# Even-odd token order, DMA transposes of keys and queries, and half of the normalising on ScalarE

## The chip, the core and the metric

The kernel runs on one core of one Trainium2 chip. The core has a matrix engine (TensorE, PE in the profile, its weight loads PEld), a vector engine (VectorE, DVE), a scalar engine (ScalarE, ACT), GpSimd (POOL) and SyncE (SP), which here only issues transfers. Sixteen DMA engines move the data. SP and ACT issue transfers on hardware queues, POOL on a software queue. Each engine works through its instructions in order and waits at an instruction until what it needs is there.

The metric is the device time of one execution in microseconds, median of several runs. Before the change it is 180.32 us (three runs, 180.05 to 180.48).

## The reference

Two stages follow one another. The first is attention over 4 batches of 8 heads, 768 tokens and 64 values a head. A token sees the 128 tokens that end with itself, and the first four tokens of the sequence (the sinks). The second is a gated block over the attention's output, 512 wide:

```python
keep = is_sink | in_window
scores = np.where(keep, scale * q @ k.T, -1e9)
a = softmax(scores);  x = a @ v                  # [B, S, 512] over the heads

h = gelu(x @ w_in);  u, v = halves of h          # 2 x 512
v_n = (v - mean(v)) / sqrt(var(v) + 1e-6) * g_ln
v_s = einsum('ts,bsd->btd', w_sg, v_n) + b_sg[None, :, None]
out = x + (u * v_s) @ w_out
```

The matrix `w_sg` (768 x 768) mixes tokens, so it and `b_sg` follow the order in which the kernel keeps the tokens.

## The kernel before

Two heads form a pair, and there are 16 pairs, four for each batch. Step n of the main loop (L571) scores pair n, while it also finishes pair n-1 and prepares pairs n+1 and n+2. All engines' orders are written out by hand: what the code issues first, an engine does first. There is no planner with costs; the only freedom is a list of fillers (below).

**Loads.** `load_qk` (L75) has SP load keys and queries of a pair, two transfers of 384 KB, in pieces of 1536 bytes (six consecutive tokens to a partition). There are two buffers of each. `load_v` (L85) has POOL load the values, 128 tokens to a tile, in pieces of 256 bytes, cast to bf16 on the way, into one of four buffers. `load_first` (L91) loads the first pair in halves on SP and ACT. `load_weights` (L159) is called at the start of each step: w_in in steps 0 to 3, w_sg in step 4, b_sg, g_ln and w_out in step 5, all on POOL's queue.

**Preparing a pair.** `repack` (L187) has POOL cast k and q to bf16 (`k_bf`, `q_bf`), two steps ahead. `keys` (L208) and `queries` (L216) turn them: six transposes of 128x128 on PE into PSUM (`cps`, L197), then one ACT copy into `kT` or `qT` (L204), which also puts the tokens back into order, since six consecutive tokens had lain in one partition. POOL then copies the sinks' keys from `kT` into `sk` (L214). In step n, `keys(n+1)` stands after the first scores, and `queries(n+1)` beside it up to step 3 and after the second scores from step 4 on. `prepare_first` (L221) does the same for pair 0 in halves.

**Attention.** `score` (L249) does a third of the scores of a pair on PE and their exp on ACT (L264); `keep_band` (L266) multiplies with a mask on DVE; `sinks` (L273) does the scores against the sinks. The score tiles have two PSUM buffers in all. `values` (L288) multiplies with v one token tile at a time; three tiles share one PSUM buffer `av`, of which there is one, and DVE normalises them together, a reciprocal (L315) and a multiply of 557 ns (L316) into `x`. The values of pair n-1 are done in step n.

**Turning x.** For pairs 4 to 6, 8 to 10 and 12 to 14 (`by_dma`, L280) SP issues a DMA transpose of x into `xT` (L321). The others are turned on PE and copied by DVE (`columns`, L283).

**The gated block.** After step 4, 8 and 12, `hidden` (L422) does the first matrix product of the batch that is finished (`hidden_v`, `hidden_u`), with gelu on ACT, and with half of the values of pair n in between. In the step after it, the second scores and `values` of the other half follow. It also fills the list `fillers`: after step 4 six `spatial_weights` (L177; PE turns w_sg by 128x128 blocks, DVE copies into `wsgT`), and for each batch eight `spatial` (L377; six matmuls `vs`, then on DVE `gv`, which needs g_ln and b_sg, and `gT`) and six `project` (L391; `o_ps`, then a DVE add or ACT copy and a store on SP). `spread` takes fillers off the list one or two at a time between the parts of steps 5 to 8 and so on. PSUM has two buffers for `vs`, `o_ps` and the hidden layers together.

After step 15 come the last values, the last hidden layer and the last batch's spatial and output products. A guard at the end checks the reciprocals' range and jumps to a slower, stable path (`stable_path`) if one is out of range; it is not run here.

Of the kernel before, what the change touches and what calls it, by code (L numbers as in the profile page):

```python
# [17 lines left out]
def kernel(  # L18
# [27 lines left out]
    assert 0 < n_sink <= 32  # L46
# [17 lines left out]
    NV = 4  # L64
    v_bufs = [consts.tile([128, 2, NT, 65], BF16, name=f"v_sb{i}") for i in range(NV)]
    kT_bufs = [consts.tile([128, S], BF16, name=f"kT{i}") for i in range(NB)]
    sk_bufs = [consts.tile([128, 128], BF16, name=f"sk{i}") for i in range(NB)]
    exs_bufs = [consts.tile([128, NS], BF16, name=f"exs{i}") for i in range(NB)]
# [6 lines left out]
    def load_qk(n):  # L75
        b, hp = divmod(n, HP)
        pair = []
        for src, name in ((k, "k_sb"), (q, "q_sb")):
            dst = loads.tile([128, 2, NT, 64], F32, name=name)
            nc.sync.dma_start(out=dst, in_=src[b, 2 * hp:2 * hp + 2].rearrange(  # L80
                "h (p t) d -> p h t d", t=NT))
            pair.append(dst)
        qk[n] = pair

    def load_v(n):  # L85
        b, hp = divmod(n, HP)
        nc.gpsimd.dma_start(  # L87
            out=v_bufs[n % NV][:, :, :, 0:64],
            in_=v[b, 2 * hp:2 * hp + 2].rearrange("h (t p) d -> p h t d", p=128))

    def load_first():  # L91
        pair = [loads.tile([128, 2, NT, 64], F32, name=name) for name in ("k_sb", "q_sb")]
        for a in range(2):
            for src, dst, queue in ((k, pair[0], nc.sync), (q, pair[1], nc.scalar)):
                queue.dma_start(
                    out=dst[:, :, HT * a:HT * (a + 1), :],
                    in_=src[0, 0:2, NH * a:NH * (a + 1)].rearrange(
                        "h (p t) d -> p h t d", t=HT))
# [10 lines left out]
    def band(dst):  # L109
        nc.gpsimd.memset(dst, 1.0)  # L110
        nc.gpsimd.affine_select(
            out=dst[:, 0:128], in_=dst[:, 0:128], compare_op=ALU.is_ge, fill=0.0,
            base=0, pattern=[[1, 128]], channel_multiplier=-1)
        nc.gpsimd.affine_select(
            out=dst[:, 128:256], in_=dst[:, 128:256], compare_op=ALU.is_ge, fill=0.0,
            base=-1, pattern=[[-1, 128]], channel_multiplier=1)
# [7 lines left out]
    for i in range(NB):  # L124
        nc.vector.memset(sk_bufs[i], 0.0)

    def copy_masks():
        nc.vector.tensor_copy(mask0, mask)
        for hl in range(2):
            nc.vector.memset(mask0[0:n_sink, 2 * hl, :], 1.0)  # L130
# [22 lines left out]
    g_sb = consts.tile([128, KU], F32, name="g_sb")  # L153
    b_bc = consts.tile([128, S], F32, name="b_bc")
    wsg_sb = consts.tile([128, NT, S], BF16, name="wsg_sb")
    w_out_sb = consts.tile([128, KU, DM], BF16, name="w_out_sb")
    wsgT = consts.tile([128, NT, S], BF16, name="wsgT")

    def load_weights(n):  # L159
# [6 lines left out]
        elif n == 4:  # L166
            for c in (slice(0, HT), slice(HT, NT)):
                nc.gpsimd.dma_start(
                    out=wsg_sb[:, c, :],
# [508 lines left out]
```

## Time and profile before

| | us |
|---|---|
| median of three runs | 180.32 |
| the profiled execution | 180.66 |
| its span in the profile | 178.8 |
| PE busy | 156.6 |
| DVE busy | 146.0 |
| ACT busy | 119.4 |
| POOL busy | 57.5 |

All times below are microseconds from the start of the span. The stages are: the first pairs up to 33, the first hidden layer up to 45.5, steps 5 to 8 up to 75, the second hidden layer up to 87, steps 9 to 12 up to 113, the third hidden layer up to 125.5, steps 13 to 15 up to about 141, then the last values, hidden layer, spatial and output products.

A line of the timeline or of the chain begins with its start and its length. The chain of waits follows the work that ended last back to the start, at each step to what released it. In a line such as "x2" the instructions of a group are merged. "SPq" and "DMA_DIRECT2D" on POOL are the time in which the engine issues a transfer, not the time in which the data moves; "to landing" counts from the issue to the last byte.

### The profile page before, as it was taken

Reading aid. Unit: us, or ns where it says so; the run is one execution under the profiler, and the core shown is the slowest. Engines: PE = TensorE matmul, PEld = TensorE weight load, DVE = VectorE, ACT = ScalarE, POOL = GpSimd, SP = SyncE. Lnnn points to the kernel's source line nnn. Section 1 sums busy time; section 2 is a strip of 40 time slices with the busy share of each in tenths; the row PEclk is TensorE's granted clock in tenths of the full one; section 3 lists DMA queues with packets and bytes.
Section 4 is the critical chain, followed back from the end, with each engine's and each line's share of the span. In section 5 each row is a group of like instructions: output and inputs, shape, how many; then the busy total and the mean of one; then the engine's idle time right before and its main releaser. Section 6 shows DMA issues by size and latency. Waiting matters only on the chain.

```text
span 178.8 us, 3744 instructions
## 1 busy us (share of the span) xinstructions
PE 156.6 (88%) x1407; PEld 88.7 (50%) x1418; DVE 146.0 (82%) x359; ACT 119.4 (67%) x168; POOL 57.5 (32%) x98
## 2 busy tenths in 40 slices
PE   0769779799689999899899999899799999999970
PEld 0447556345556555445456545355465554555430
DVE  5665989599889999698999998699999948858950
ACT  2488999867938668666968668877986856640000
POOL 8459999950042060425006070550010000000000
PEclk9999999999999999999999999999999999999999
DMA  5999999999857739895285969986202241011072
GB/s 158 266 306 265 267 271 273 191 207 218 103 179 48 202 66 209 303 270 39 20 219 33 214 183 192 380 108 44 44 4 44 50 178 59 0 63 60 0 294 66
DMA packets 47974, 27.24 MB, mean 152 GB/s; under 512 B 33680, under 2 KB 44944, under 8 KB 47952
## 3 DMA queue, kind: packets, MB, share of 16 engines
q0 software_dynamic: 27904, 6.31, 37.5%
q1 hardware_dynamic: 19504, 20.26, 37.5%
q10 hardware_dynamic: 544, 0.39, 0.7%
q8 instruction: 12, 0.20, 0.5%
q14 instruction: 10, 0.08, 0.1%
HBM read 24.81 MB, written 6.29 MB: 174 GB/s over the span
## 4 chain that ended last, share of the span: by engine, by line
PE 75%; ACT 12%; issue 4%; DVE 4%; DMA 2%
PE vs L383 17%; PE hu L345 13%; PE o_ps L397 11%; PE hv L333 11%; ACT ex L264 7%; PE sc L260 7%; PE cps L197 5%; PE av L305 4%; ACT kT L204 3%; PE scs L275 2%; PE av L308 2%; DMA k_sb<-in_k_dram 2%; ACT qT L204 2%; PE av L311 1%; DVE ex L271 1%
## 5 line engine op out<-in xcount | busy, mean ns | idle before, releaser
L264 ACT ACTIVATE ex<-sc 128x1024 bf16<-128x1024 f32 (+1 forms) x48 | 45.6, 958 | 16.9 <-PE sc L260 16.7
L383 PE MATMUL vs<-wsgT,vn 128*128 128x384 bf16 x192 | 35.5, 327 | 0.5 <-DVE wsgT L182 0.4
L191 POOL CAST k_bf<-k_sb 128x768 bf16<-128x768 f32 x15 | 12.3, 823 | 42.7 <-DMA k_sb<-in_k_dram 31.8
L397 PE MATMUL o_ps<-w_out_sb,gT 128*128 128x512 bf16 (+1 forms) x93 | 23.8, 370 | 1.2 <-DVE o_sb L401 0.8
L271 DVE TENSOR_TENSOR ex<-ex,mask 128x1024 bf16<-128x1024 bf16 x32 | 23.0, 722 | 1.8 <-ACT ex L264 1.7
L333 PE MATMUL hv<-w_in_sb,xT 128*128 128x512 bf16 x92 | 22.2, 379 | 1.9 <-DVE xT L286 1.7
L383 PEld LDWEIGHTS <-vn 128*128 128x128 bf16 x192 | 17.9, 98 | 12.0 <-issue 1.2
L345 PE MATMUL hu<-xT,w_in_sb 128*128 128x384 bf16 x128 | 23.2, 325 | 0.1
L260 PE MATMUL sc<-qT,kT 64*128 64x256 bf16 x192 | 19.0, 280 | 2.2 <-DVE qT L240 1.3
L386 DVE SCALAR_TENSOR_TENSOR gv<-vs,g_sb,b_bc 128x384 bf16<-128x384 f32 x32 | 19.5, 611 | 1.7 <-PE vs L383 1.7
L348 ACT ACTIVATE uT<-hu 128x384 bf16<-128x384 f32 x32 | 15.7, 490 | 6.5 <-PE hu L345 6.3
L337 DVE BATCH_NORM_STATS2 st<-v_all 128x6 f32<-128x512 f32 x24 | 16.3, 677 | 4.6 <-ACT v_all L335 4.5
L335 ACT ACTIVATE v_all<-hv 128x512 f32<-128x512 f32 x24 | 14.3, 597 | 7.2 <-PE hv L333 6.9
L316 DVE TENSOR_TENSOR x<-av,inverses 128x384 bf16<-128x384 f32 x32 | 17.8, 557 | 1.1
L305 PE MATMUL av<-v_sb,ex 128*128 128x65 bf16 x192 | 18.2, 198 | 0.2 <-DVE x L316 0.2
L305 PEld LDWEIGHTS <-ex 128*128 128x128 bf16 x192 | 14.5, 100 | 7.2 <-issue 2.9
L345 PEld LDWEIGHTS <-w_in_sb 128*128 128x128 bf16 x128 | 12.4, 97 | 10.7 <-issue 2.9
L87 POOL DMA_DIRECT2D v_sb<-in_v_dram x16 | 16.6, 1036 | 0.0
L308 PE MATMUL av<-v_sb,ex 128*128 128x65 bf16 x160 | 16.5, 197 | 0.0
L214 POOL COPY sk<-kT 64x4 bf16<-64x4 bf16 x30 | 6.2, 207 | 28.2 <-ACT kT L204 27.3
L191 POOL CAST q_bf<-q_sb 128x768 bf16<-128x768 f32 x15 | 14.1, 938 | 3.0 <-DMA q_sb<-in_q_dram 2.2
L333 PEld LDWEIGHTS <-xT 128*128 128x128 bf16 x96 | 9.0, 98 | 11.9 <-DVE xT L286 2.6
(83 smaller groups left out, 241.4 us busy)
## 6 DMA issues: line engine op xcount, KB each, us to landing
k_sb<-in_k_dram SPq DMA_DIRECT2D x15, 384.0 KB, 5.5
q_sb<-in_q_dram SPq DMA_DIRECT2D x15, 384.0 KB, 6.1
out_dram<-o_sb SPq DMA_DIRECT2D x17, 256.0 KB, 3.5
v_sb<-in_v_dram POOLq DMA_DIRECT2D x16, 192.0 KB, 6.9
out_dram<-o_act SPq DMA_DIRECT2D x6, 256.0 KB, 2.0
wsg_sb<-in_moe_w_sg_dram POOLq DMA_DIRECT2D x2, 576.0 KB, 10.2
w_in_sb<-in_moe_w_in_dram POOLq DMA_DIRECT2D x4, 256.0 KB, 8.9
w_out_sb<-in_moe_w_out_dram POOLq DMA_DIRECT2D x1, 512.0 KB, 11.8
```

Source lines behind the costliest of these rows:

```text
L191: eng.tensor_copy(flat.rearrange("p t (h d) -> p h t d", h=2), src)
L260: nc.tensor.matmul(sc[:, hl, w:w + n_q], kT[rows, 128 * j:128 * (j + 1)], qT[rows, 128 * j:128 * j + n_q], start=True, stop=True)
L264: nc.scalar.activation(out=part, in_=sc[:, :, 0:w], func=AF.Exp, scale=scale)
L271: nc.vector.tensor_mul(part, part, m)
L305: nc.tensor.matmul(av[:, m, hl, :], probs(i, hl, 0), v_sb[:, hl, i, :], start=(m == 0 and hl == 0), stop=False)
L308: nc.tensor.matmul(av[:, m, hl, :], probs(i - 1, hl, 1), v_sb[:, hl, i - 1, :], start=False, stop=False)
L316: nc.vector.tensor_mul(x_sb[b][:, hp, HT * c:HT * (c + 1), :].rearrange("p i (h d) -> p i h d", h=2), av[:, :, :, 0:64], rcp.to_broadcast( ...
L333: nc.tensor.matmul(h_ps, xT[b][:, c, 128 * j:128 * (j + 1)], w_in_sb[:, c, DF:], start=(c == 0), stop=(c == KD - 1))
L345: nc.tensor.matmul(h_ps[:, 0:NH], w_in_sb[:, c, 128 * f:128 * (f + 1)], xT[b][:, c, NH * n:NH * (n + 1)], start=(c == 0), stop=(c == KD - 1))
L383: nc.tensor.matmul(vs[:, 0:NH], vns[b][:, si, 128 * f:128 * (f + 1)], wsgT[:, si, cols], start=(si == 0), stop=(si == NT - 1))
L386: nc.vector.scalar_tensor_tensor(out=gv, in0=vs[:, 0:NH], scalar=g_sb[:, f:f + 1], in1=b_bc[:, cols], op0=ALU.mult, op1=ALU.add)
L397: nc.tensor.matmul(o_ps, gTs[b][:, c, rows], w_out_sb[:, c, cols], start=(c == 0), stop=(c == KU - 1 and whole))
```

## The change

The tokens are kept in another order: of each 256 tokens, a partition p holds tokens 2p and 2p+1. Keys and queries are loaded so, in pieces of 512 bytes; values, masks, the weights w_sg and b_sg and the output follow that order. Block j of the scores is now picked out of `kT` and `qT` by `key_block` and `query_blocks`. `kT` is kept in two halves.

For pairs 6 to 15, `turn` replaces `keys` and `queries`: SP issues three DMA transposes, two for the halves of `kT` and one for `qT`, straight from `k_bf` and `q_bf`, at the start of the step before. Pairs 1 to 5 are still turned on PE, both in the same place.

The sinks' keys come from one POOL multiply with a constant `own`. The second `av` tile of pairs 6 and up takes the PSUM buffer that the transposes leave free. For the second half of eight pairs (5, 6, 7, 9, 10, 11, 13, 14) ACT multiplies with the reciprocals, in six instructions of 64 columns each, instead of DVE's one.

w_sg's columns and b_sg are brought into the new order by POOL copies (`wsg_p` in step 4, `b_bc` in step 5). v, w_sg and each output tile take two transfers of 64 partitions instead of one of 128 (or of half the columns). The DVE's output tiles have five buffers instead of six.

```diff
@@ load_qk @@
             nc.sync.dma_start(
-                out=dst, in_=src[b, 2 * hp:2 * hp + 2].rearrange("h (p t) d -> p h t d", t=NT))
+                out=dst.rearrange("p h (g t) d -> p (h g) (t d)", t=2),
+                in_=src[b, 2 * hp:2 * hp + 2].rearrange(
+                    "h (g p t) d -> p (h g) (t d)", p=128, t=2))
@@ load_v @@
-        nc.gpsimd.dma_start(
-            out=v_bufs[n % NV][:, :, :, 0:64],
-            in_=v[b, 2 * hp:2 * hp + 2].rearrange("h (t p) d -> p h t d", p=128))
+        for t in range(2):
+            nc.gpsimd.dma_start(
+                out=v_bufs[n % NV][64 * t:64 * t + 64, :, :, 0:64],
+                in_=v[b, 2 * hp:2 * hp + 2].rearrange(
+                    "h (j p t) d -> t p h j d", p=64, t=2)[t])
@@ load_first: k in parts of 256 and 512 tokens, q of 512 and 256, one transfer for each 256 @@
+                for g in range(*first_part(src, a)):
+                    queue.dma_start(
+                        out=dst[:, :, 2 * g:2 * g + 2, :].rearrange("p h t d -> p h (t d)"),
+                        in_=src[0, 0:2, 256 * g:256 * g + 256].rearrange(
+                            "h (p t) d -> p h (t d)", t=2))
@@ band: four selects of 64 partitions instead of two of 128 @@
...
@@ load_weights @@
         elif n == 4:
-            for c in (slice(0, HT), slice(HT, NT)):
+            for t in range(2):
                 nc.gpsimd.dma_start(
-                    out=wsg_sb[:, c, :],
-                    in_=moe_w_sg.rearrange("(c p) s -> p c s", p=128)[:, c, :])
+                    out=wsg_sb[64 * t:64 * t + 64],
+                    in_=moe_w_sg.rearrange("(c p t) s -> t p c s", p=64, t=2)[t])
+            nc.gpsimd.dma_start(out=b_row, in_=moe_b_sg.partition_broadcast(128))
         elif n == 5:
-            nc.gpsimd.dma_start(out=b_bc, in_=moe_b_sg.partition_broadcast(128))
             nc.gpsimd.dma_start(out=g_sb, ...)
             nc.gpsimd.dma_start(out=w_out_sb, ...)
@@ new @@
+    def sink_keys(n):
+        kT, sk = kT_bufs[n % NB], sk_bufs[n % NB]
+        first = kT[:, 0:128].rearrange("c (t p) -> c p t", t=2)[:, 0:n_sink // 2, :]
+        nc.gpsimd.tensor_mul(sk..., first..., own...)
+
+    def turn(n):
+        qTs[n] = work.tile([128, S], BF16, name="qT")
+        k_bf, q_bf = packed.pop(n)
+        for h in range(2):
+            nc.sync.dma_start_transpose(
+                out=halves(kT_bufs[n % NB])[:, h],
+                in_=k_bf[64 * h:64 * h + 64].rearrange("p i d -> p (i d)"))
+        nc.sync.dma_start_transpose(
+            out=qTs[n].rearrange("c (i p) -> c i p", i=NT),
+            in_=q_bf.rearrange("p i d -> p (i d)"))
+        sink_keys(n)
@@ score @@
-                nc.tensor.matmul(sc[:, hl, w:w + n_q], kT[rows, 128 * j:128 * (j + 1)],
-                                 qT[rows, 128 * j:128 * j + n_q], start=True, stop=True)
+                nc.tensor.matmul(sc[:, hl, w:w + n_q], key_block(kT, rows, j),
+                                 query_blocks(qT, rows, j), start=True, stop=True)
@@ values @@
-            avs[n] = ps_a.tile([128, HT, 2, 65], F32, name="av", tag="av")
+            pool, tag = (ps_t, "tp") if c == 1 and n > PET else (ps_a, "av")
+            avs[n] = pool.tile([128, HT, 2, 65], F32, name="av", tag=tag)
...
+            if c == 1 and n >= HP and n % HP > 0 and n < NP - 1:
+                for t in range(HT):
+                    for hl in range(2):
+                        nc.scalar.activation(out=x[:, t, hl], in_=av[:, t, hl, 0:64],
+                                             func=AF.Copy, scale=rcp[:, t, hl])
+            else:
+                nc.vector.tensor_mul(x, av[:, :, :, 0:64], rcp.to_broadcast([128, HT, 2, 64]))
@@ project @@
-            o_sb = small.tile([128, DM], F32, name="o_sb", bufs=6)
+            o_sb = small.tile([128, DM], F32, name="o_sb", bufs=5)
...
-        queue.dma_start(out=out[b, rows, cols], in_=o_sb[:, cols])
+        for i in range(2):
+            queue.dma_start(out=out[b, rows, cols].rearrange("(p t) d -> t p d", t=2)[i],
+                            in_=o_sb[64 * i:64 * i + 64, cols])
@@ main loop, PET = 5 @@
         load_weights(n)
+        if n == HP + 1:
+            G.tensor_copy(b_bc.rearrange("p (j t c) -> p j t c", t=2, c=64),
+                          b_row.rearrange("p (j c t) -> p j t c", t=2, c=64))
+        if PET <= n < NP - 1:
+            turn(n + 1)
+        if n == HP:
+            for ti in range(NT):
+                G.tensor_copy(wsg_p[:, ti].rearrange("p (j t c) -> p j t c", t=2, c=64),
+                              wsg_sb[:, ti].rearrange("p (j c t) -> p j t c", t=2, c=64))
...
-            if g == 0 and n > 0 and n + 1 < NP:
+            if g == 0 and 0 < n < PET:
                 keys(n + 1)
-                if n < HP:
-                    queries(n + 1, A, ps_m, "mm")
+                queries(n + 1, A, ps_m, "mm")
...
-            if g == 1 and n + 1 < NP and n >= HP:
-                queries(n + 1, A, ps_t, "tp")
```

## The prediction

> **What bounds the kernel now.** I read the page's busy shares and its chain first, then the windows by stage, then the chain inside one pair step (step n is the pass of the main loop that scores pair n), and last the queues of POOL and SP, because the change moves work onto both.
>
> ```profile
> PE 156.6 (88%) x1407; PEld 88.7 (50%) x1418; DVE 146.0 (82%) x359; ACT 119.4 (67%) x168; POOL 57.5 (32%) x98
> PE 75%; ACT 12%; issue 4%; DVE 4%; DMA 2%
> 8.00:33.00 25.00, 19.64 (x252) 13.60 (x253) 19.04 (x47) 22.79 (x31) 22.20 (x32) 1.00 1.46 267
> 87.00:113.00 26.00, 24.57 (x246) 13.24 (x246) 24.70 (x51) 20.20 (x26) 6.70 (x12) 1.00 0.75 160
> ```
>
> The last two lines are windows: start:end, length, then busy time of PE, PEld, DVE, ACT and POOL, clock, DMA share, GB/s. The first pairs (8 to 33 us) are not PE's: ACT (22.8 of 25 us), POOL (22.2) and DMA (share 1.46) are all full. From step 5 on, PE is full, but DVE is fuller still (24.70 against 24.57 of 26 us). The hidden layers (33 to 45.5, 75 to 87, 113 to 125.5) and the tail from 146 are PE's and the diff leaves them alone.
>
> Step 7, in the chain:
>
> ```profile
> 60.01 0.32 PE sc L260 x4
> 60.80 0.34 PE cps L197 x6
> ...
> 63.08 0.34 PE cps L197 x6
> ...
> 66.71 0.32 PE sc L260 x4
> ...
> 87.33 1.02 ACT ex L264
> 88.35 0.70 ACT kT L204
> 89.05 0.04 issue
> 89.10 0.49 PE cps L197 x6
> ```
>
> The two cps lines are the key and query transposes of one pair: 0.68 us of a step of 6.70 us, on the path. The last four lines are step 9, behind a hidden layer: PE waits for ACT's kT copy before it may transpose queries.
>
> **The part of the trace that I fear** is POOL's order around the spatial weights, with DVE's first use of them:
>
> ```profile
> 31.30 1.50 POOL L168 DMA_DIRECT2D wsg_sb<-in_moe_w_sg_dram  x2
> ...
> 33.31 0.82 POOL L191 CAST k_bf<-k_sb 128x768 bf16<-128x768 f32 x1
> ...
> 34.98 1.04 POOL L87 DMA_DIRECT2D v_sb<-in_v_dram  x1
> ...
> 36.56 0.77 POOL L173 DMA_DIRECT2D g_sb<-in_moe_g_ln_dram  x1
> 37.30 0.78 POOL L174 DMA_DIRECT2D w_out_sb<-in_moe_w_out_dram  x1
> DMA to landing us min/median/max: 9.1/10.2/11.2
> 52.15 0.62 DVE L386 SCALAR_TENSOR_TENSOR gv<-vs,g_sb,b_bc 128x384 bf16<-128x384 f32 x1 [0.76 <-PE vs L383]
> ```
>
> The landing line is that of wsg_sb: the second half, issued at 32.05, lands at 43.25. Nobody on POOL waits for it now; POOL runs ahead and issues the loads of g_sb and w_out 15 us before gv wants them.
>
> **Part by part, in span time.**
>
> *Gains after step 6.* Pairs 6 to 15 lose 12 transposes (0.68 us of PE) and two ACT copies (0.79 and 0.81). ACT gets, for eight pairs, six 64-column copies: its PSUM copies take 578 ns for 512 columns and 372 for 256, so 0.80 ns a column and 166 fixed, 217 each, 1.3 a pair (bounds: 202 each, the 1x1 activation's row, and 372). DVE loses one 557 ns x per such pair. A second av buffer (the freed tp bank) ends the wait "PEld L305 <- DVE x L316", 1.9 us in all. Steps 7, 10 and 11 are held by PE and DVE alike: -0.6, -0.6, -0.65. Step 8 and 12 end in exp, keep_band and the xT copy (111.09, 111.93, 112.49 in the chain), and that exp now stands behind ACT's six copies, which wait for DVE's reciprocal: -0.3 and -0.1. Steps 9 and 13 lose the kT wait; gv is next late: -0.75 each. Step 14, whose next score waits for the late exp's buffer: -0.4. Step 15: 0. Sum **-4.15**. Bounds: -6.0 (eight times 0.68 and 0.3 at steps 9 and 13) and -2.5 (six DVE-held steps at 0.4).
>
> *The POOL queue at steps 4 and 5.* Now wsg_p's six copies wait for wsg's landing, and behind them in order stand sk(5), the casts of pair 7, v(7) in two issues, g_sb, w_out, the copy into b_bc, sk(6), and the casts and v of pair 8. wsg_p: no bf16 copy of 128x768 is in the trace; the nearest are the casts, 0.82 alone and up to 1.29 beside DVE; I take 0.90, 5.4 in all (4.9 to 7.7). sk 0.25 (0.2 to 0.45). Casts 1.65. v in halves: 768 descriptors each, between w_out's 512 (0.78) and the whole v's 1536 (1.04): 0.84 each, 1.7 (1.0 to 2.1). g_sb 0.77, w_out 0.78, b_bc 0.85 (0.82 to 1.3). Sum 11.4 from wsg's landing to the first possible gv.
>
> When does wsg land? All loads before it run on full DMA engines from 4.5 us on, and k and q now come in 512-byte pieces instead of 1536. Rows: xT's transposes, about 250 bytes a packet, ran at 213 GB/s; k and q at 350 to 430 in the windows around 92 us; the first halves, 768 bytes beside 1536, at 362. By the line between 250 and 1536 bytes a pair's 2.1 us become 2.7, so 4.9 over eight pairs; by the 768-byte row, 0. I take 1.6, nearer the 768-byte row, which is the same kind of transfer: wsg lands at 44.85. Ends: 48.1, and 42.0, which excludes no gain: POOL issues the second half at 35.5, after 0.45 us more in each of six steps, and the quickest load of w_in landed in 6.5. gv can start at 56.25 instead of 52.15. DVE stands there with gT, x and keep_band of step 6 queued behind it; PE has both vs banks full, does sc and av of step 6 and stops. Its third vs starts at 56.9 instead of 54.21; then its av waits until DVE has done gv, gT, gv, gT, the reciprocal and x (58.9), so the fourth vs starts at 59.55 instead of 56.49: **+3.1** (-0.3 to +6.5). That takes up whatever steps 0 to 5 gain or lose by less: in those, POOL's step of 4.25 us grows by 0.65 (v twice) less 0.2 (one sk multiply for two copies of 207 ns), which its lead of 1.4 to 2 us over PE's transposes covers; late k and q of pair 2 cost some 0.8 there.
>
> The Trainium skill ("DMA: Bandwidth & Descriptors", Why small descriptors are slow) counts three extra bus cycles a packet: 3x19 against 51 cycles is 12%, by my estimate 2.0 us over eight pairs where I took 1.6. The same page (Rules for kernel authors) advises against two transfers for two partition halves, as they share the engines; no row here shows it, and by it v's and the output's halves would gain nothing and cost their issues.
>
> *Turned pairs that come late.* SP now issues, at the start of step n, two kT halves and qT of pair n+1. They wait for PE's sinks of step n-1, behind SP's own loads:
>
> ```profile
> 57.20 1.28 SPq L321 DMA_TRANSPOSE xT<-x  x1
> 58.57 0.53 SPq L80 DMA_DIRECT2D k_sb<-in_k_dram  x1
> 59.20 0.42 SPq L80 DMA_DIRECT2D q_sb<-in_q_dram  x1
> ```
>
> Pair 8's would start at 60 and take SP 1.2 for qT and 0.6 to 1.2 for each half; the q load ahead of them lands at 63.5; then 393 KB at 213 GB/s take 1.85, so 65.4, or 66.5 if a half costs as much as a whole; step 8 would start at 66.0. Pairs 6, 7, 9, 10, 13 and 14 have a stall or a hidden layer between, 11's load goes out 2 us earlier (89.78), 15 has none ahead. So two pairs (8 and 12) may be late by 0 to 1.5: **+1.3** (0 to 3). xT, the next loads and stores move behind these issues; the casts' lead of one step covers them.
>
> *Tail.* Each store becomes two issues. The last four come at 173.25 and after; one more 0.35 us issue lies before the last landing: **+0.35** (0 to 0.7).
>
> *At nothing:* four mask selects for two (0.29 each; POOL idles 0.85 before its first cast), six first loads for four (a 0.47 issue more on ACT, which idles 1.74 before its first kT copy), own's and mask0's memsets, and o_sb's five buffers for six (landing 2 to 7 us covers four adds in a row; without that, up to 1 us at step 8).
>
> Sum: -4.15 + 3.1 + 1.3 + 0.35 = +0.6: span 179.4. The profiled run took 180.66 for a span of 178.8, 0.34 above the median of 180.32; so **180.9** in the median.
>
> **Rivals.**
> 1. *Faster: POOL's chain is in time.* wsg lands at 42.0 and its copies take 0.82: gv at about 53.0, shift -0.2, sum -2.7, 177.6. For it: POOL idles 9.2 us before 47.28. Against: DMA is full until 49. It decides at a first gv of 55.6; earlier is faster.
> 2. *The small loads bound the first pairs.* All 4.9 us fall due: wsg at 48.1, gv at 59.5, shift +6.4, sum +3.9: 184.2. For it: DMA share 1.46; q of pair 6 lands 0.3 us before its cast. Against: 362 GB/s with 768 bytes.
> 3. *Transposes late in every step.* 1.5 us at five more pairs: +7.5, 188. Against: xT lands in 2.8 us when alone.
> 4. *DVE holds every step.* Gains -2.5: 182.5.
> 5. *Transposes stay on PE:* excluded, the order of PE's instructions has 120 fewer.
>
> **How the numbers follow.** 0.2% is 0.36 us, about what this kernel's measurement can tell from no change. Forecast (first gv 55.0 to 58.5, the rest as summed) 0.38; rival 1 0.35; rival 2 0.13; rival 3 0.05; rival 4 0.09. Rival 1 and the forecast's low end give faster 0.39; a strip of 0.72 us inside the forecast gives same 0.09; the rest is slower, 0.52. The range has to take in rivals 1, 2 and 4: rival 1 with 0.8 of its best gains is 176.8, rival 2 with 1 us of late transposes more is 185.2. The likeliest case alone: 179.7 to 183.2.
>
> **What would show it.** First gv near 56 with a wait for POOL or g_sb of some 4 us, and POOL waiting for wsg_sb before six copies: right; gv near 52 to 53: rival 1. Steps 7, 10 and 11 at 6.1 us: the gains. Score waits on qT or kT from DMA at steps 8 and 12 only: the third term; at every step: rival 3. Casts of pairs 2 to 6 waiting for DMA above the 2.4 us of pair 2 now: rival 2. I am wrong throughout if steps 7 to 14 don't shorten.

## The result and the profile after

The changed kernel takes 204.3 us in the median (203.3 to 204.8) against 180.4 before: 1.131 times as long, interval 1.125 to 1.137. The profiled execution took 203.74 us, with a span of 202.0. The forecast was 180.9 with an upper end of 185.2. Here and below, executions in which the core ran visibly slower than in the others of the same kernel are left out of ranges and ratios, and where the profiled one is such, its stage times stand as "-".

Five differences of the two traces make up the 23.2 us of span:

| from, to | before | after | more |
|---|---|---|---|
| start to the first score of pair 5 | 43.6 | 54.0 | 10.4 |
| from there to pair 7's | 16.3 | 23.1 | 6.8 |
| to pair 8's | 6.7 | 7.5 | 0.8 |
| to the last layer's first `vs` | 92.7 | 95.6 | 2.9 |
| to the end of the span | 19.4 | 21.8 | 2.3 |

The page of the changed kernel, busy time and chain:

```profile
PE 159.3 (79%) x1298; PEld 84.9 (42%) x1298; DVE 144.9 (72%) x356; ACT 114.7 (57%) x196; POOL 69.8 (35%) x107
DMA 30%; DVE 24%; PE 24%; ACT 10%; POOL 3%; SPq 2%; issue 2%; POOLq 0%; DVEq 0%; ACTq 0%
```

DMA had 2% of the chain and now has 30%; PE fell from 75% to 24%. The windows say where (start:end, length, busy time of PE, PEld, DVE, ACT and POOL, clock, DMA share, GB/s); the first and the last answer the two shown of before:

```profile
8.00:33.00 25.00, 17.35 (x218) 11.85 (x219) 17.94 (x42) 19.03 (x25) 18.21 (x26) 1.00 1.71 203
33.00:54.00 21.00, 15.27 (x104) 7.58 (x101) 13.79 (x39) 11.87 (x19) 6.37 (x10) 0.92 1.82 168
54.00:77.00 23.00, 16.73 (x140) 9.63 (x139) 13.12 (x25) 9.74 (x16) 14.56 (x20) 0.78 0.90 125
101.00:127.00 26.00, 22.13 (x200) 11.20 (x199) 21.47 (x49) 16.67 (x30) 11.20 (x15) 0.98 1.21 176
```

From 8 to 33 us the DMA engines are busier than before (share 1.71, was 1.46) and move less (203 GB/s, was 267), and all five engines work less for it. From 54 to 77 no engine is near full: something is waited for. POOL's queue shows it (start, length, engine, line; in brackets the idle time before and who ended it):

```profile
31.07 0.83 POOL L210 CAST q_bf<-q_sb 128x768 bf16<-128x768 f32 x1 [2.14 <-DMA q_sb<-in_q_dram]
33.35 0.74 POOL L183 DMA_DIRECT2D w_in_sb<-in_moe_w_in_dram  x1
...
38.89 1.35 POOL L188 DMA_DIRECT2D wsg_sb<-in_moe_w_sg_dram  x2
...
56.82 5.13 POOL L657 COPY wsg_p<-wsg_sb 128x768 bf16<-128x768 bf16 x6 [15.75 <-DMA wsg_sb<-in_moe_w_sg_dram]
...
64.04 1.54 POOL L92 DMA_DIRECT2D v_sb<-in_v_dram  x2
65.57 0.80 POOL L193 DMA_DIRECT2D g_sb<-in_moe_g_ln_dram  x1
```

```profile
DMA to landing us min/median/max: 15.2/16.2/17.1
```

```profile
70.23 0.62 DVE L445 SCALAR_TENSOR_TENSOR gv<-vs,g_sb,b_bc 128x384 bf16<-128x384 f32 x1 [4.80 <-DMA g_sb<-in_moe_g_ln_dram]
```

The first of these two is wsg_sb's landing, the second the first `gv` in VectorE's timeline. The last piece of w_in goes out 6.3 us later than before (33.35, was 27.04), because the cast ahead of it waits for queries; w_sg lands 16.2 us after its issue in place of 10.2, at 56.8; then come the six copies, and g_sb's load waits behind them and is itself waited for.

The lateness of pair 5 is in the chain of the changed kernel: the queries, then the last piece of w_in, for which the hidden layer waits. In the chain of before, the same matmuls of the hidden layer wait for no load:

```profile
21.08 9.84 DMA q_sb<-in_q_dram
...
33.35 13.76 DMA w_in_sb<-in_moe_w_in_dram
...
47.15 6.91 PE hu L404 x30
```

```profile
38.01 0.65 PE hu L345 x4
...
38.69 4.99 PE hu L345 x28
```

Step 7 and the start of step 8, in the chain:

```profile
74.53 1.34 ACT x L374 x6
75.86 0.70 ACT ex L314
76.56 0.46 ACT exs L328
...
77.15 4.54 DMA k_sb<-in_k_dram
81.69 2.80 DMA qT<-q_bf
84.49 0.14 issue
84.62 0.40 PE sc L310 x4
```

The exponential stands behind ACT's six copies, and pair 8's query transpose, which SP issues behind the key load and the two halves of `kT`, lands at 84.5; PE's scores wait for it. At the end SP issues twice as many stores:

```profile
190.09 6.28 SPq L469 DMA_DIRECT2D out_dram<-o_sb  x10
196.46 1.66 SPq L469 DMA_DIRECT2D out_dram<-o_act  x2
198.21 1.19 SPq L469 DMA_DIRECT2D out_dram<-o_sb  x2
```

Ten halves take 6.28 us of issue where five tiles took 3.94 before:

```profile
169.21 3.94 SPq L409 DMA_DIRECT2D out_dram<-o_sb  x5
```

### The profile page after: what moved, and what is told of

It reads as the page before. It is cut to its first block, busy times and chain, and to the rows that moved or that the text cites. A ratio compares the mean times of both kernels' runs of the same rounds, so it can differ in the third digit from the quotient of the medians.

```text
span 202.0 us, 3651 instructions
## 1 busy us (share of the span) xinstructions
PE 159.3 (79%) x1298; PEld 84.9 (42%) x1298; DVE 144.9 (72%) x356; ACT 114.7 (57%) x196; POOL 69.8 (35%) x107
## 4 chain that ended last, share of the span: by engine, by line
DMA 30%; DVE 24%; PE 24%; ACT 10%; POOL 3%; SPq 2%; issue 2%; POOLq 0%; DVEq 0%; ACTq 0%
DMA q_sb<-in_q_dram 15%; DMA w_in_sb<-in_moe_w_in_dram 7%; PE o_ps L456 7%; PE hu L404 6%; ACT x L374 4%; PE vs L442 4%; DVE vn L432 4%; DVE gv L445 4%; DVE st L396 3%; DVE ex L321 3%; DMA qT<-q_bf 3%; PE hv L392 3%; ACT ex L314 3%; DVE x L377 2%; DVE gT L448 2%
## 5 line engine op out<-in xcount | busy, mean ns | idle before, releaser
L442 PE MATMUL vs<-wsgT,vn 128*128 128x384 bf16 x192 | 37.1, 336 | 2.9 <-DVE gv L445 1.5
L210 POOL CAST k_bf<-k_sb 128x768 bf16<-128x768 f32 x15 | 13.2, 883 | 53.3 <-DMA k_sb<-in_k_dram 40.7
L404 PE MATMUL hu<-xT,w_in_sb 128*128 128x384 bf16 x128 | 24.8, 342 | 3.6 <-DMA w_in_sb<-in_moe_w_in_dram 3.5
L321 DVE TENSOR_TENSOR ex<-ex,mask 128x1024 bf16<-128x1024 bf16 x32 | 24.3, 761 | 3.2 <-ACT ex L314 3.2
L456 PE MATMUL o_ps<-w_out_sb,gT 128*128 128x512 bf16 (+1 forms) x100 | 25.2, 380 | 1.5 <-DVE o_sb L460 1.2
L442 PEld LDWEIGHTS <-vn 128*128 128x128 bf16 x192 | 18.3, 100 | 16.4 <-issue 5.0
L92 POOL DMA_DIRECT2D v_sb<-in_v_dram x32 | 24.6, 776 | 0.0
L407 ACT ACTIVATE uT<-hu 128x384 bf16<-128x384 f32 x32 | 15.7, 490 | 11.6 <-PE hu L404 11.4
L396 DVE BATCH_NORM_STATS2 st<-v_all 128x6 f32<-128x512 f32 x24 | 16.3, 679 | 5.6 <-ACT v_all L394 5.6
L368 DVE RECIPROCAL inverses<-av 128x6 f32<-128x6 f32 x32 | 6.0, 187 | 15.1 <-PE av L364 15.1
L210 POOL CAST q_bf<-q_sb 128x768 bf16<-128x768 f32 x15 | 13.3, 887 | 8.2 <-DMA q_sb<-in_q_dram 6.0
L310 PEld LDWEIGHTS <-kT 64*128 64x128 bf16 x192 | 6.3, 97 | 21.4 <-issue 18.2
L456 PEld LDWEIGHTS <-gT 128*128 128x128 bf16 x100 | 9.3, 99 | 11.2 <-issue 4.3
## 6 DMA issues: line engine op xcount, KB each, us to landing
wsg_sb<-in_moe_w_sg_dram POOLq DMA_DIRECT2D x2, 576.0 KB, 16.2
```

The costliest lines, as they stand in the source:

```text
L92: nc.gpsimd.dma_start(out=v_bufs[n % NV][64 * t:64 * t + 64, :, :, 0:64], in_=v[b, 2 * hp:2 * hp + 2].rearrange("h (j p t) d -> t p h j d" ...
L210: eng.tensor_copy(flat.rearrange("p t (h d) -> p h t d", h=2), src)
L310: nc.tensor.matmul(sc[:, hl, w:w + n_q], key_block(kT, rows, j), query_blocks(qT, rows, j), start=True, stop=True)
L321: nc.vector.tensor_mul(part, part, m)
L396: nc.vector.bn_stats(out=st, in_=v_alls[b][:, j, :])
L404: nc.tensor.matmul(h_ps[:, 0:NH], w_in_sb[:, c, 128 * f:128 * (f + 1)], xT[b][:, c, NH * n:NH * (n + 1)], start=(c == 0), stop=(c == KD - 1))
```

## The experiments

All ratios are against the kernel before on the same chip. Stage times are from one profiled execution each. Executions of the changed kernel and its variants scatter by 1 to 3%; where two profiles have the same code up to pair 5, its start differs by up to 4 us (53.0 in e10, 57.0 in e6).

| run | ratio (interval) | pair 5 | pair 5 to 7 | pair 8 to end |
|---|---|---|---|---|
| before | 1 | 43.6 | 16.3 | 112.2 |
| changed | 1.131 (1.125 to 1.137) | 54.0 | 23.1 | 117.4 |
| e1 | 1.098 (1.092 to 1.103) | - | - | - |
| e2 | 1.09 to 1.11 (two executions) | 51.7 | 23.0 | 117.4 |
| e3 | 1.118 (1.109 to 1.126) | 52.1 | 21.1 | 118.7 |
| e5 | 1.078 (1.066 to 1.089) | 44.8 | 24.1 | 117.5 |
| e4 | 1.013 (1.010 to 1.016) | 46.7 | 16.3 | 112.0 |
| e16 | 1.044 (1.036 to 1.052) | 50.5 | 16.4 | 112.1 |
| e17 | 1.065 (1.058 to 1.071); the profiled execution 1.045 | 51.2 | 16.4 | 112.1 |
| e18 | 1.014 (1.011 to 1.018) | 45.3 | 16.3 | 111.8 |
| e6 | 1.12 (two executions) | 57.0 | 16.2 | 118.7 |
| e8 | 1.027 (1.020 to 1.034) | 43.7 | 16.3 | 116.1 |
| e10 | 1.106 (1.099 to 1.112) | 53.0 | 24.0 | 113.1 |
| e19 | 1.024 (1.021 to 1.028) | 43.5 | 16.3 | 115.2 |
| e13 | 1.015 (1.006 to 1.023) | 48.6 | 16.7 | 110.4 |
| e9 | 1.027 (1.018 to 1.035) | - | - | - |
| e11 | 1.520 (1.512 to 1.527) | 52.5 | 17.7 | 194.3 |
| e14 | 1.095 (1.088 to 1.102) | - | - | - |
| e15 | 1.079 (1.068 to 1.089) | - | - | - |
| e12 | 1.141 (1.136 to 1.147) | - | - | - |

**The loads, taken back one at a time in the changed kernel.** Theories A to D: 512-byte pieces, 64-partition halves, the transposes of pair 6, the order of POOL's work.

e1, keys and queries in pieces of 1536 bytes:

```diff
-                out=dst.rearrange("p h (g t) d -> p (h g) (t d)", t=2),
-                in_=src[b, 2 * hp:2 * hp + 2].rearrange(
-                    "h (g p t) d -> p (h g) (t d)", p=128, t=2))
+                out=dst, in_=src[b, 2 * hp:2 * hp + 2].rearrange("h (p t) d -> p h t d", t=NT))
```

> The changed kernel, with the loads of keys and queries of pairs 1 to 15 back in pieces of 1536 bytes; the tokens of those pairs then stand in another order than the masks and the weights take them, so it does not compute the reference, and the work is otherwise the same. Theory A (the three times as many packets of these loads are what the saturated transfers of the first 50 us can't take): the first score of pair 5 returns from 53.99 us to 46 to 49, the third piece of the input weights lands 9 to 11 us after its issue (13.8 in the changed kernel), and the time is 192 to 197 us. Theories B (64-partition transfers on the software queue), C (the transposes of pair 6) and D (the order of POOL's weight work): within 2 us of 204.3, pair 5 still at 52 or later.

e2, values and w_sg whole in their partitions:

```diff
-        for t in range(2):
-            nc.gpsimd.dma_start(
-                out=v_bufs[n % NV][64 * t:64 * t + 64, :, :, 0:64],
-                in_=v[b, 2 * hp:2 * hp + 2].rearrange(
-                    "h (j p t) d -> t p h j d", p=64, t=2)[t])
+        nc.gpsimd.dma_start(
+            out=v_bufs[n % NV][:, :, :, 0:64],
+            in_=v[b, 2 * hp:2 * hp + 2].rearrange("h (t p) d -> p h t d", p=128))
...
-                    out=wsg_sb[64 * t:64 * t + 64],
-                    in_=moe_w_sg.rearrange("(c p t) s -> t p c s", p=64, t=2)[t])
+                    out=wsg_sb[:, c, :],
+                    in_=moe_w_sg.rearrange("(c p) s -> p c s", p=128)[:, c, :])
```

> The changed kernel, with each pair's values loaded by one transfer of 128 partitions and the spatial weights by two transfers of 128 partitions and half the columns, as before the change; values and spatial weights then lie in another order than the rest takes them, so it does not compute the reference. Theory B (the halves of 64 partitions crowd the software queue and land late): pair 5's first score at 48 to 51 us, the spatial weights land 10 to 12 us after their issue (15 to 17 in the changed kernel), time 197 to 201 us. Theories A, C and D: within 1.5 us of 204.3, less the 0.7 us of issue that POOL saves in a step where POOL decides.

e3, no turning by DMA:

```diff
-    PET = 5
+    PET = 15
```

> The changed kernel with no DMA transposes of keys and queries: TensorE turns all sixteen pairs, ScalarE copies them, and the second half's values take the one bank as before the change; it computes the reference. Theory C (the transposes of pair 6 crowd the weights' landings at 35 to 47 us, and those of pairs 7, 8 and 12 come late): pair 5's first score at 49 to 51 us, the late scores of pairs 8 and 12 gone, time 195 to 199 us although TensorE and ScalarE have their work back. Theories A and B: pair 5 unchanged at 53 to 54 us; then the gain from the late scores (some 4 us) and the work that comes back (5 to 7 us in ten steps) about cancel: 203 to 208 us.

Each gave back 1 to 4% and moved pair 5 by 1.3, 2.3 and 1.9 us, which is no more than the scatter: none is the cause alone. PE's wait for w_in, 7.3 us in the changed kernel and none before, was 6.6 us in e2 and 2.8 in e3, and the spatial weights still landed 11 to 14 us after their issue. e5 has all three edits.

> The changed kernel with all three of the former edits together: keys, queries, values and spatial weights loaded in the pieces of the kernel before, no DMA transposes of keys and queries. The order of the tokens is then not the one that masks and weights take, so it does not compute the reference; the weights' rearranging on POOL, ScalarE's normalising and the split stores stay. Each edit alone moved pair 5's first score from 53.99 us to 52.69, 51.66 and 52.08. Theory F (one shared supply, the DMA engines of the first 50 us, of which each edit gives back its part): the three add up, pair 5's first score at 47 to 49 us, time 190 to 195 us. Rival G (what holds pair 5 isn't the transfers' form but POOL's own work): pair 5 at 51 or later, time 197 us or more.

Pair 5 starts at 44.8, 9.2 of the 10.4 us earlier: G falls, and F's shared supply holds. But the parts don't add as F has it: singly they gave 5.5 us in all. It fits that what one edit frees, the others fill. The 9.2 are of one execution: e13 below has the same loads, and pair 5 at 48.6. So the parts have to be put into the kernel before, where nothing else crowds.

**The loads, put into the kernel before.** e4 is e1's diff turned round, e16 is e2's turned round, e17 has both. e4, the 512-byte pieces:

```diff
-            nc.sync.dma_start(out=dst, in_=src[b, 2 * hp:2 * hp + 2].rearrange(
-                "h (p t) d -> p h t d", t=NT))
+            nc.sync.dma_start(
+                out=dst.rearrange("p h (g t) d -> p (h g) (t d)", t=2),
+                in_=src[b, 2 * hp:2 * hp + 2].rearrange(
+                    "h (g p t) d -> p (h g) (t d)", p=128, t=2))
```

> The kernel before, with only the loads of keys and queries of pairs 1 to 15 in the changed kernel's pieces of 512 bytes; the order of its tokens is then not the masks' one, so it does not compute the reference. Theory A: pair 5's first score moves from 43.60 us to 50 to 53, and the time is 187 to 191 us. Theories B, C and D: within 1.5 us of 180.4, pair 5 before 45.5.

e16, the halves of 64 partitions:

```diff
-            out=v_bufs[n % NV][:, :, :, 0:64],
+                out=v_bufs[n % NV][64 * t:64 * t + 64, :, :, 0:64],
...
-                    out=wsg_sb[:, c, :],
+                    out=wsg_sb[64 * t:64 * t + 64],
```

> The kernel before, with only its values and spatial weights loaded in halves of 64 partitions as in the changed kernel; their order is then another than the rest takes, so it does not compute the reference. Theory B alone: pair 5's first score moves from 43.60 us to 45.5 to 48, time 182.5 to 185. If the halves only cost POOL's issues (0.5 us a step, less than POOL's lead): within 1 us of 180.5.

e17, both diffs:

> The kernel before, with keys and queries in 512-byte pieces and values and spatial weights in halves of 64 partitions; it does not compute the reference (order of tokens). The 512-byte pieces alone moved pair 5's first score by 3.1 us. If the two costs add: pair 5 at 48.5 to 51, time 185 to 188. If they grow on each other, as the changed kernel without transposes suggests (52.08): pair 5 at 51.5 to 54, time 188.5 to 192.

The 512-byte pieces cost 1.3%, a third of what theory A wanted; pair 5 is 3.1 us later. The halves cost 4.4% (180.1 to 188.0 us) and pair 5 6.9 us: more than their theory asked. Both cost 6.5% (4.5% in the profiled execution; the four took 188.25 to 193.22 us), and pair 5 comes at 51.2, 7.6 us later where the two alone made 10.0. That lies between the two expectations and is nearly the changed kernel's 54.0. The software queue's line of the page (packets, MB, share of 16 engines' span), of before and then of e16:

```profile
q0 software_dynamic: 27904, 6.31, 37.5%
```

```profile
q0 software_dynamic: 28160, 6.31, 47.3%
```

And the window from 6 to 29 us, again before and e16:

```profile
6.00:29.00 23.00, 18.31 (x227) 12.60 (x226) 17.11 (x44) 20.11 (x27) 19.02 (x28) 1.00 1.48 264
```

```profile
6.00:29.00 23.00, 16.75 (x206) 11.48 (x205) 16.12 (x41) 18.73 (x25) 19.26 (x28) 1.00 1.61 217
```

The same bytes in nearly as many packets take 87.8 us of all engines (47.3% of 185.7) in place of 67.1, and the rate of everything falls from 264 to 217 GB/s. Not all of this need be the halves' own price, since a packet's time also stretches with what runs beside it: e17, with the same halves, shows 77.4 us, and e13, without any, 77.1. In e16's chain a value load stands for 12.91 us:

```profile
24.97 0.71 POOL v_sb L88
25.68 12.91 DMA v_sb<-in_v_dram
38.59 0.14 issue
38.99 1.71 PE hv L335 x4
```

Is it the half partitions or the second transfer? e18 loads by head, two transfers of 128 partitions:

```diff
-        nc.gpsimd.dma_start(
-            out=v_bufs[n % NV][:, :, :, 0:64],
-            in_=v[b, 2 * hp:2 * hp + 2].rearrange("h (t p) d -> p h t d", p=128))
+        for hl in range(2):
+            nc.gpsimd.dma_start(out=v_bufs[n % NV][:, hl, :, 0:64],
+                                in_=v[b, 2 * hp + hl].rearrange("(t p) d -> p t d", p=128))
```

> The kernel before, with each pair's values loaded by two transfers again, but one for each head, each over all 128 partitions (the halves of 64 partitions cost 7.5 us in e16 with the spatial weights'); it computes the reference. If it is the half partitions that cost: pair 5's first score within 1.5 us of 43.60 and 180 to 182 us. If it is the number of transfers and POOL's second issue: pair 5 at 48 to 51 and 185 to 189 us.

1.4%, pair 5 at 45.3, 257 GB/s in the same window: just outside the first expectation and far from the second. The second transfer costs 2.4 us, the half partitions the other 5.5 of e16's 7.9. In these 5.5 are w_sg's halves, and that each of e16's transfers reads every second token's 256 bytes where e18's read all of a head's; no run takes these apart.

The Trainium skill ("SBUF — State Buffer", Can I just issue two DMAs to hit both halves?) says that two transfers on the two partition halves run one after the other, and that only one transfer over all 128 partitions reaches all of SBUF's ports. e16 against e18 agrees in kind: 188.0 against 182.5 us.

**The copies of w_sg.** e6 drops POOL's seven copies:

```diff
-            for ti in range(NT):
-                G.tensor_copy(wsg_p[:, ti].rearrange("p (j t c) -> p j t c", t=2, c=64),
-                              wsg_sb[:, ti].rearrange("p (j c t) -> p j t c", t=2, c=64))
...
-            nc.tensor.transpose(wps[:, si, :], wsg_p[:, ti, 128 * si:128 * (si + 1)], iden)
+            nc.tensor.transpose(wps[:, si, :], wsg_sb[:, ti, 128 * si:128 * (si + 1)], iden)
...
-            nc.gpsimd.dma_start(out=b_row, in_=moe_b_sg.partition_broadcast(128))
+            nc.gpsimd.dma_start(out=b_bc, in_=moe_b_sg.partition_broadcast(128))
```

> The changed kernel without POOL's seven copies that rearrange the spatial weights and their bias; TensorE turns the weights as they landed and the bias is broadcast straight into its place, so columns stand in the wrong order and it does not compute the reference. Theory D (the copies are in the chain between the weights' landing and the first gating): the first gating moves from 70.23 us to 63 to 65 us, pair 7's first score from 77.08 to 71 to 73, time 197 to 200 us. Rival (the copies fill a wait that pair 7's late keys would leave anyway): first gating at 67 us or later, time 202 us or more.

The total hardly moved, 202.4 and 202.8 us, and the first gating came at 66.12: neither expectation fits. In this execution pair 5 itself came 3.0 us later, on code that up to there is the same. The stage is clear: pair 5 to pair 7 takes 16.2 us, as before the change, and every kernel of the table without the copies takes 16.2 to 17.7, every one with them 21.1 to 24.1. e5 against e8 says the same: pair 5 starts at 44.8 and 43.7, both have ScalarE's normalising, and the stage takes 24.1 with the copies (e5) and 16.3 without (e8). The copies cost about 7 us; of what e6 gained there, 3.0 us went to its late pair 5, 1.1 to the step before pair 8, where the chain waits 3.65 us for a query transpose (2.80 in the changed kernel), and 1.2 to what follows. How much of that is scatter is open.

**ScalarE's normalising.** e8 puts it alone into the kernel before:

```diff
+            if c == 1 and n >= HP and n % HP > 0 and n < NP - 1:
+                for t in range(HT):
+                    for hl in range(2):
+                        nc.scalar.activation(out=x[:, t, hl], in_=av[:, t, hl, 0:64],
+                                             func=AF.Copy, scale=rcp[:, t, hl])
+            else:
```

> The kernel before, with only ScalarE's normalising of the second half's values in eight pairs, 6 instructions for one of VectorE; it computes the reference. Theory: TensorE carries these steps (9.9 of 10 us busy in the steps around 60 us) and ScalarE has the room for 1.3 us more a pair, so the time stays at 179.5 to 182. Rival: VectorE is what the hidden layers wait for, and 0.56 us less of it in six steps shows: 177 to 179. Other rival: ScalarE's scores come behind the normalising and each of the eight steps grows by its 1.3 us: 186 to 191.

e10 takes it alone out of the changed one:

```diff
-            if c == 1 and n >= HP and n % HP > 0 and n < NP - 1:
+            if False:
```

> The changed kernel with all normalising on VectorE again (the rest of the change stays; it computes the reference). On the kernel before, ScalarE's normalising alone cost 5.1 us. Theory H (the step's last exponential waits behind six copies that wait for VectorE's reciprocal, in every step of this kind): 4 to 5.5 us come back, 198.5 to 200.5 us, and from pair 8's first score to the end of the span 112.5 to 114 us in place of 117.4. Rival (these steps are held by late keys and VectorE anyway in the changed kernel): 202 us or more.

It costs 2.7% alone, 4.6 us of span, all after pair 7; taking it out gives 4.3 us back between pair 8 and the end. Both fit theory H. VectorE's wait for the exponentials, of before, e8 and e19 (total, times, longest):

```profile
DVE ex L271 <- ACT ex L264: 3.0, 7, 0.8
```

```profile
DVE ex L271 <- ACT ex L264: 11.4, 13, 1.4
```

```profile
DVE ex L271 <- ACT ex L264: 4.7, 12, 0.8
```

And e8's chain in step 7, now a ring through VectorE, ScalarE and back:

```profile
64.36 0.12 DVE inverses L315
64.48 0.02 issue
64.50 1.34 ACT x L321 x6
65.84 0.69 ACT qT L204
66.53 0.72 ACT ex L264
67.25 0.02 issue
67.28 0.56 DVE ex L271
```

e19 keeps the copies, collects them (and x's transpose behind them) in a list, and issues them after the step's third exponential:

```diff
+            if g == 2:
+                while later:
+                    later.pop(0)()
```

> The kernel before, with ScalarE's normalising of half the values of eight pairs (5.1 us slower in e8), its six copies moved behind the step's third exponential in ScalarE's order; it computes the reference. Theory H (the cost is the exponential that waits behind the copies, and VectorE's masking behind that): the wait of VectorE for the exponentials falls from 11.4 us to under 5 and the time to 179 to 181.5. Rival (the copies' own 1.3 us a step is what costs, or the bank of the values that is held longer): 183.5 to 187.

Most of the wait is gone, and pair 12 starts at 106.49 as in the kernel before (106.54; e8: 109.06). Yet the whole is 2.4% slower than before, inside the rival's range. 1.1 us come between pairs 12 and 13, with the third hidden layer (18.2 us, 17.1 before): PE's transposes of x, which this layer needs, now wait for the late copies, 1.2 us in three waits, of which the first is

```profile
112.31 0.23 PE L197 MATMUL cps<-iden,x 128*128 128x128 bf16 x1 [0.83 <-ACT x L330]
```

2.0 come after pair 15, where `av` of the next values waits for the copies (0.51 and 0.73 us) and ScalarE's `o_act` stands behind them (at 145.99, 143.07 before). So the wait for the exponential explains the loss up to pair 12, 2.5 of e8's 4.6 us, but moving the copies doesn't save the rest: whatever needs x or its bank then waits for them.

**The transposes, and what is left.** e13 keeps the DMA transposes, the order of scores and the second bank: it has the edits of e1, e2, e6 and e10, and whole stores. e9 is e5 and e6 together with whole stores, so that ScalarE's normalising is left. The stores:

```diff
-        for i in range(2):
-            queue.dma_start(out=out[b, rows, cols].rearrange("(p t) d -> t p d", t=2)[i],
-                            in_=o_sb[64 * i:64 * i + 64, cols])
+        queue.dma_start(out=out[b, rows, cols], in_=o_sb[:, cols])
```

> The changed kernel with former loads, stores and weights (no rearranging, no ScalarE normalising), and with the DMA transposes of ten pairs kept: of the change, the transposes, the order of scores and masks and the second bank for values are left. The order of tokens doesn't fit, so it does not compute the reference. If the transposes pay what the forecast gave them (-0.3 to -0.75 a step, less 1.3 for late pairs): 177 to 179.5 us. If they crowd the weights' landings and come late for pairs 8 and 12: pair 5's first score at 46 to 49 us, time 181.5 to 186.

> The last two together, and the output stores in one piece of 128 rows each: of the change, the even-odd order of scores and masks and ScalarE's normalising of half the values of eight pairs are left. It does not compute the reference (the order of tokens and of columns doesn't fit). If loads, rearranging, transposes and stores carry the whole loss: 179 to 184 us, pair 5's first score at 44 to 48. If ScalarE's normalising or the new masks cost something that no profile line named yet: 186 us or more, with pair 5 at 47 or earlier. The end after the last value product of the fourth hidden layer is 19.4 us as before (21.7 in the changed kernel) if the split stores made it longer.

e9's ratio is e8's, within its interval: loads, transposes, copies and stores carry all the rest. In e13 pair 8 to the end takes 110.4 us, 1.8 less than before, and the tail after the last `vs` is 19.1 (19.4 before, 21.8 with split stores). The transposes do pay there, but about half of what was forecast. The whole is 1.5% slower, in the profiled execution because pair 5 comes 5.0 us late. That isn't shown to be the transposes': PE waits up to 30.63 for values that took 11.57 us in the chain, and SP issues the first transpose of keys only then:

```profile
19.02 11.57 DMA v_sb<-in_v_dram
```

```profile
34.47 2.63 SPq L242 DMA_TRANSPOSE kT<-k_bf  x2
```

What delayed these values, which e5 loads in the same way, is open. The transposes' price on the DMA engines, before and e13:

```profile
q1 hardware_dynamic: 19504, 20.26, 37.5%
```

```profile
q1 hardware_dynamic: 36096, 24.19, 57.8%
```

105.5 us of all engines (57.8% of 182.6) less 67.1 is 38.5 for ten pairs, 3.85 a pair. PE's transposes of a pair took 0.68 us.

**Mended kernels.** e11 computes the reference with no copies (PE takes the columns of w_sg at stride 2), VectorE's normalising, transposes from pair 9 on, and each tile stored by one transfer whose source is 128 partitions and whose target is two sets of 64 rows. e14 splits the stores again; e15 also turns all pairs on PE.

```diff
+                nc.tensor.transpose(
+                    wps[64 * t:64 * t + 64, si, :],
+                    wsg_sb[:, ti].rearrange("p (j c t) -> p j t c", t=2, c=64)[:, si, t], iden)
...
-    PET = 5
+    PET = 8
...
+        queue.dma_start(out=out[b, rows, cols].rearrange("(p t) d -> t p d", t=2), in_=o_sb[:, cols])
```

> The changed kernel, mended where it still computes the reference: no copies of the spatial weights (TensorE takes their columns at stride 2, in two transposes of 64 columns for one of 128), all normalising on VectorE, whole output stores, DMA transposes from pair 9 on only. The 512-byte loads and the halves of 64 partitions stay, since the order of tokens wants them. By the parts measured (pair 5's first score at about 52 us without the transposes of pair 6, 16.3 us from there to pair 7, 110 to 113 us from pair 8 to the end): 185 to 191 us. If the parts don't add up, above all if the crowded first 50 us don't get better without pair 6's transposes: 193 us or more.

> The mended kernel with its output stores split in two again (one store whose rows go to every second row was landing at 51 GB/s with a DMA share of 0.13); it computes the reference. No copies of the spatial weights, all normalising on VectorE, transposes from pair 9 on. If only those stores spoiled the mended kernel: 187 to 193 us, with pair 5's first score at 52 to 54, 16 to 18 us from there to pair 7, and 110.5 to 113.5 us from pair 8 to the end. If the stride-2 transposes or the late start of the DMA transposes cost something themselves: 195 us or more.

> The same, with all sixteen pairs turned on TensorE; it computes the reference. If DMA transposes pay once the weights have landed: 1.5 to 4 us slower than with them from pair 9 on, all of it after pair 8. If they cost as much as they save: within 1 us of it.

e11 took 274.7 us. Near its end nothing but one store after the other was left, in this window:

```profile
246.00:251.00 5.00, 0.00 (x0) 0.00 (x0) 0.00 (x0) 0.00 (x0) 0.00 (x0) 0.50 0.13 52
```

52 GB/s at a share of 0.13: two of sixteen engines. With split stores 1.095, without turning 1.079. Both are above what the parts gave, so these don't add here either. Transposing late doesn't pay: without it (e15) the time is some 3 us less, which neither expectation had, though the two intervals just touch. e17's loads alone are 1.065 (1.045 at the least), so about half or more of both is the loads that the token order asks for. No mended kernel beats the one before, and none with e13's plain loads that computes the reference was tried.

e12 is the changed kernel once more, for the scatter.

> The changed kernel as it is, once more, for how much its crowded first 55 us vary from one execution to the next: time 202.5 to 206 us; pair 5's first score at 52 to 57 us (53.99 before; 57.03 in the kernel without the rearranging, which has the same loads); from there to pair 7's 22 to 24 us.

206.0 us, 1% above the first measurement.

## Why the prediction was wrong

**The POOL queue at steps 4 and 5 (+3.1): mechanism right, landing mis-sized by 12 us.** POOL's own work after w_sg's landing took 11.2 us (11.4 forecast); a copy into `wsg_p` took 0.86 (0.90), a half of v 0.77 of issue (0.84). The first `gv` came 13.4 us after the landing, since it waited for g_sb, whose load of 4.53 us after its issue the sum left out. But w_sg landed at 56.8, not at 44.85, and `gv` came at 70.23, not 56.25. Against before, w_sg's landing is 13.6 us later: it was issued 7.6 later, and the transfer took 6.0 more. The failing step is the cost of the halves of 64 partitions: the forecast gave v's halves their issues alone, 1.7 us on POOL, and no transfer time, though DMA was full. e16, the halves alone, starts pair 5 6.9 us late; against e18 it puts 5.5 us of the whole time on the half partitions and 2.4 on the second transfer. The rule that the forecast cited speaks against halves, but was read as pricing their issues only.

**The 512-byte pieces (1.6, ends 0 and 4.9)** cost 3.1 us at pair 5 (e4): inside its bounds. Rival 2 named the right place but only this one cause; its upper end held 4.9 us where both forms cost 7.6 (e17).

**"Takes up whatever steps 0 to 5 gain or lose."** POOL's lead of 1.4 to 2 us was to cover them. It was used up: pair 5 was 10.4 us late before the copies began. Two costs that were treated as covering each other came one after the other, 10.4 and 6.8.

**Gains after step 6 (-4.15): sign wrong.** The forecast let ScalarE's six copies delay an exponential only in steps 8, 12 and 14, still counted gains of 0.3, 0.1 and 0.4 there, and took VectorE's 557 ns as saved. The same order holds in every step with the copies: e8 shows +4.6, of which 0.6 each at steps 7 and 11, 1.2 and 1.1 at 8 and 12, 0.3 at 14 and 0.7 after it; steps 6 and 10 lose nothing. The transposes' own part was half right: e13 has -0.4 at steps 9 and 13 (-0.75 each forecast), -0.7 at 14 (-0.4), -0.6 and -0.7 at 8 and 12 (-0.3 and -0.1), but +0.1, +0.2 and +0.6 at 7, 10 and 11 (-0.6, -0.6, -0.65). Steps 7 and 10 are held by VectorE, rival 4's case: e13's chain there is VectorE's, and 42% DVE in all. Step 11 ends in a wait for pair 12's query transpose, which the chain has for 4.36 us:

```profile
107.27 4.36 DMA qT<-q_bf
```

**Late transposes (+1.3, ends 0 and 3): about right.** Pairs 8 and 12, as forecast: +0.8 and +2.5 with ScalarE's delay in them, +0.4 and +1.0 without it (e10). Their price was not: 393 KB were taken at 213 GB/s, 1.85 us, and cost 3.85 us of all engines.

**Tail (+0.35): +2.3.** One more issue before the last landing was counted. A half costs SP 0.63 us of issue where a whole tile cost 0.79, and the issues of ten halves queue before the last ones.

## What to carry to other kernels

Where the DMA engines are full, a new token order is paid in the form of its transfers: ask of each load how many partitions it covers before how long its pieces are, and look at the engine time of its queue (packets' share times span) beside the landings, knowing that it also stretches with what runs beside it. Work that moves to an engine with idle time still stands in that engine's order: look for what stands behind it in a step, and who waits for that. Costs of several edits to one saturated supply don't add in either direction, so put each alone into the quiet kernel.

## What the hardware showed unasked

A store whose target is two sets of 64 rows ran on two engines (0.13 of 16, 52 GB/s). The Trainium skill ("DMA: Bandwidth & Descriptors", Rules for kernel authors) has it that an outermost dimension smaller than 16 confines a transfer to at most as many engines; e11 agrees, with its outermost of 2.

PE's granted clock was 0.50 from 58 to 68 us, while POOL copied w_sg and what came behind it; PE had stood still for 2.68 us before the first transpose of w_sg. The twelve `vs` matmuls there, 2.11 us before the change, took 3.61. The chain of waits doesn't go through them: `gv` waited for g_sb until 70.23. A window and a line of PE's timeline, and the line of before:

```profile
58.00:68.00 10.00, 8.45 (x53) 5.08 (x52) 5.34 (x9) 2.42 (x3) 10.00 (x14) 0.50 0.82 127
```

```profile
65.02 3.61 PE L442 MATMUL vs<-wsgT,vn 128*128 128x384 bf16 x12
```

```profile
50.97 2.11 PE L383 MATMUL vs<-wsgT,vn 128*128 128x384 bf16 x12 [0.40 <-DVE wsgT L182]
```
